# Writing five engines' instructions into the main body instead of into a block

## The chip, the cores and the metric

The kernel runs on one core of one Trainium2 chip. The metric is device time in microseconds (us); lower is better. The core has five engines that run instruction streams of their own and meet only through semaphores: TensorE (PE, with its weight loads shown as PEld), VectorE (DVE), ScalarE (ACT), GpSimd (POOL) and SyncE (SP), which here issues transfers.

## The reference, cut to what matters

Two independent problems, A and B, of the same shape are computed and their outputs laid side by side. Each is one decoding step of attention over the last 4096 positions of a cache.

```python
B, Sq, D = 2, 1, 576
Hq, Hkv, Sk, Dh = 32, 16, 16384, 128
W = min(4096, max(256, Sk // 4))                      # 4096
q = (x @ wq).reshape(B, Sq, Hq, Dh).transpose(0, 2, 1, 3)
k = jnp.repeat(k_cache[:, :, Sk - W:, :], 2, axis=1)
v = jnp.repeat(v_cache[:, :, Sk - W:, :], 2, axis=1)
p = softmax(jnp.einsum("bhqd,bhkd->bhqk", q, k) * Dh ** -0.5)
o = jnp.einsum("bhqk,bhkd->bhqd", p, v)
out = o.transpose(0, 2, 1, 3).reshape(B, Sq, Hq * Dh) @ wo     # 2 x 1 x 576
# result: concatenate([out_A, out_B], axis=-1), 2 x 1 x 1152, bfloat16
```

## The kernel before, in words

The caches are cut into slabs of 4 MB (128 partitions of 16384 bfloat16): 16 slabs of keys and 16 of values for both problems together. A ring of four slab buffers (`ring`) holds what is in flight. SP issues nearly all loads, in a written order: the two query weights `wq` (L253, L255), then key and value slabs in turn (L246), with pieces of the output weights `wo` between them (L280). A slab's load waits until the last reader of its ring slot is done. The last value slab comes in two pieces (L242).

For a key slab, DVE transposes 32x32 blocks of it (L460) and PE multiplies with the queries (L483, L167); for the softmax DVE takes the maximum (L493, L506), ACT the exponential (L528), and POOL spreads the row sums (L544). For a value slab PE multiplies (L575), and ACT copies the sums out (L587). Towards the end of each problem PE multiplies with `wo` (L690) and DVE and ACT copy the halves of the result to `out_sb` (L698, L699). Four small stores write it out (L708), three from SP's queue and one from ACT's.

The order on each engine is written out by the program itself. `S.add` appends an operation with its dependencies to the list of one engine; `S.check` walks the lists; a second walk works out which semaphore values each operation has to wait for. At the end `emit(name, engine)` turns one engine's list into instructions: the waits, the operation, and the step of that engine's semaphore. Behind its list SP also waits until the four stores have landed (`out_sem`).

Before the first of these instructions there is an opening barrier that the program object makes when it is created (L893): four engines report on one semaphore, POOL gathers them and releases them on another. The kernel opens a block (L106 to L107); each engine's list is then written by a function registered with the block (L854 to L873), so that the source has, for each engine, a jump into its part of the block and one out of it, and where the block is left (recorded under L106) a second barrier of the same kind: a DRAIN on each engine, a gathering and releasing on POOL.

Of the kernel before, what the change touches and what calls it, by code (L numbers as in the profile page):

```python
# [59 lines left out]
def build_kernel(nc, probs, out, cfg=None):  # L60
# [8 lines left out]
    NPROB = len(probs)  # L69
    Bb, _one, D = x0.shape  # L70
    _, Hkv, Sk, Dh = k0.shape
    HD = wq0.shape[1]
    Hq = HD // Dh
# [30 lines left out]

    es = ExitStack()
    with es:  # L106
        block = es.enter_context(nc.Block())  # L107
        sb = lambda name, shape, dt: es.enter_context(nc.sbuf_tensor(name, shape, dt))
        ring = sb("ring", [128, NR, SLABW], BF16)
        xt = sb("xt", [128, NKT, 2048], FP32)  # L110
# [51 lines left out]
        out_sem = sem("outdone")  # L162
# [10 lines left out]
        dma_count = {}  # L173
# [672 lines left out]
        def emit(eng_name, engine):  # L846
            for op in S.ops[eng_name]:
                for s_h, val in todo[id(op)]:
                    engine.wait_ge(s_h, val)
                last = op.fn(engine)  # L850
                if op.dma is None:
                    last.then_inc(ev[eng_name], 1)

        @block.sync  # L854
        def _(e):
            emit("sp", e)
            e.wait_ge(out_sem, dma_count[out_sem])

        @block.tensor
        def _(e):  # L860
            emit("pe", e)

        @block.vector
        def _(e):
            emit("dve", e)

        @block.scalar
        def _(e):
            emit("act", e)

        @block.gpsimd
        def _(e):
            emit("pool", e)  # L873


def bass_concat_heads__sliding_block_cached__sliding_block_cached__decode_kernel(
    nc, A_x, A_k_cache, A_v_cache, A_wq, A_wo, B_x, B_k_cache, B_v_cache, B_wq, B_wo, out,
):
    build_kernel(nc, [(A_x, A_k_cache, A_v_cache, A_wq, A_wo), (B_x, B_k_cache, B_v_cache, B_wq, B_wo)], out)
# [28 lines left out]
```

## Time and profile before

| | |
|---|---|
| median of three runs | 366.08 us |
| lowest and highest of the runs | 365.82 and 366.17 us |
| span of the profiled execution, from first to last recorded instruction of the program | 364.5 us |
| the profiled execution's own time | not listed apart from its span |
| instructions recorded | 2971 |
| mean granted TensorE clock | 0.834 of full speed |
| busy: PE, DVE, ACT, POOL | 219.7, 198.6, 67.8, 16.4 us |
| HBM read | 153.10 MB, 420 GB/s over the span |

The profile is one execution on the chip, with times counted from the first recorded instruction. The first and the last microsecond matter here, and instructions that only wait, branch or step a semaphore are not counted as busy; they are found under the line of the source that made them. "SPq" and the like stand for an engine's instruction queue. The trace also keeps the moments at which semaphores change, those of the program around the kernel too, and these lie before the zero and behind the end of the span as well.

### The profile page before, as it was taken

The page shows a single profiled execution, that of the slowest core. Times are in us where ns is not written, and L with a number is a line of the kernel's source. Part 1 is how long each engine was busy: PE and PEld are TensorE (multiplying, and loading weights), DVE is VectorE, ACT ScalarE, POOL GpSimd, SP SyncE. Part 2 cuts the span into 40 slices and gives each one's busy share as a digit, 9 for nine tenths or more (in the row PEclk, how much of TensorE's full clock was granted, in tenths as well). Part 3 has the DMA queues.
Part 4 walks back from the last instruction along what each step waited for, and adds up shares of the span by engine and source line. Part 5 has one row for each costly group of instructions (what it writes and reads, how often), then busy time and mean ns, then how long its engine had stood idle before and what let it go on. Part 6 is the DMA issues. An engine that isn't in the chain of part 4 may idle for free.

```text
span 364.5 us, 2971 instructions
## 1 busy us (share of the span) xinstructions
PE 219.7 (60%) x1370; PEld 64.7 (18%) x1097; DVE 198.6 (54%) x173; ACT 67.8 (19%) x155; POOL 16.4 (4%) x45
## 2 busy tenths in 40 slices
PE   0399687291837657192955749083764828286866
PEld 0023112020211212021211212021221202021132
DVE  2022895574909375382917568291926557199620
ACT  1047203020300303020200303020210303011211
POOL 5000000000000000000000000000000000000000
PEclk9999899697885969687685969889696969869985
DMA  8999999999999999999999999999999999999993
GB/s 345 432 432 435 428 409 457 414 453 408 440 435 428 433 412 447 424 433 428 427 445 421 442 424 424 430 432 432 422 450 421 442 421 423 439 421 442 415 419 136
DMA packets 7075, 153.27 MB, mean 420 GB/s; under 512 B 780, under 2 KB 1304, under 8 KB 1688
## 3 DMA queue, kind: packets, MB, share of 16 engines
q1 hardware_dynamic: 7056, 153.10, 98.1%
q8 instruction: 9, 0.15, 0.2%
q10 hardware_dynamic: 8, 0.00, 0.0%
q14 instruction: 2, 0.02, 0.0%
HBM read 153.10 MB, written 0.00 MB: 420 GB/s over the span
## 4 chain that ended last, share of the span: by engine, by line
DMA 70%; DVE 14%; PE 12%; ACT 2%; issue 0%; SPq 0%; DVEq 0%
DMA ring<-in_B_k_cache_dram 34%; DMA ring<-in_A_k_cache_dram 25%; DVE xt L460 13%; DMA ring<-in_B_v_cache_dram 8%; PE st L483 4%; PE st L167 3%; DMA x_sb<-in_B_x_dram 3%; PE tb L413 3%; ACT qrow L422 1%; PE tb L167 1%; DVE qtr L428 1%; PE ot L690 1%; DVE nM L506 1%; ACT qk L436 0%; PE tb L496 0%
## 5 line engine op out<-in xcount | busy, mean ns | idle before, releaser
L460 DVE STREAM_TRANSPOSE xt<-ring 128x2048 f32<-128x2048 f32 x64 | 144.9, 2285 | 108.3 <-DMA ring<-in_B_k_cache_dram 59.4
L483 PE MATMUL st<-xt,zq 128*128 128x512 bf16 x256 | 113.0, 442 | 121.5 <-DVE xt L460 121.2
L167 PE MATMUL st<-xt,zq 128*128 128x512 bf16 x256 | 111.9, 437 | 0.0
L483 PEld LDWEIGHTS st<-xt,zq 128*128 128x128 bf16 x256 | 27.3, 107 | 209.7 <-DVE xt L460 138.5
L511 ACT ACTIVATE nMrep<-nM 1x128 f32<-1x128 f32 x16 | 4.9, 308 | 176.5 <-DVE nM L506 176.5
L575 PE MATMUL acc<-ring,pC 128*32 128x512 bf16 x512 | 34.1, 403 | 1.3 <-DMA ring<-in_B_v_cache_dram 1.3
L536 DVE STREAM_TRANSPOSE pC<-pR 128x1024 bf16<-128x1024 bf16 x16 | 19.4, 1214 | 3.7 <-ACT pR L528 2.1
L587 ACT ACTIVATE acc_sb<-acc 128x512 bf16<-128x512 f32 x16 | 9.5, 596 | 62.8 <-PE acc L575 62.8
L493 DVE TENSOR_REDUCE m<-st 128x1 f32<-128x1024 f32 x16 | 19.0, 1190 | 1.0 <-PE st L167 0.9
L528 ACT ACTIVATE pR<-st,bias_sb 128x1024 bf16<-128x1024 f32 x16 | 17.8, 1113 | 0.5
L413 PE MATMUL tb<-ring,xT 128*128 128x512 bf16 x50 | 16.5, 419 | 0.1
L575 PEld LDWEIGHTS acc<-ring,pC 128*32 128x32 bf16 x512 | 13.2, 100 | 17.3 <-issue 6.2
L428 DVE STREAM_TRANSPOSE qtr<-qrow 128x512 f32<-128x512 f32 x8 | 5.7, 711 | 19.1 <-ACT qrow L422 19.1
L544 POOL TENSOR_SCALAR rsel<-maskS,rsum 128x8 f32<-128x8 bf16 x16 | 4.9, 306 | 243.1 <-ACT pR L528 243.1
L391 ACT ACTIVATE st<-maskB 128x1024 f32<-128x1024 bf16 x14 | 14.4, 1028 | 0.4
L447 POOL TENSOR_TENSOR zq<-qk,maskA 128x128 bf16<-128x128 bf16 x16 | 6.3, 398 | 86.8 <-PE st L167 69.5
L690 PE MATMUL ot<-wob,Rsb 128*2 128x288 bf16 x120 | 9.8, 309 | 0.3 <-ACT Rsb L670 0.3
L422 ACT ACTIVATE qrow<-tb 128x512 bf16<-128x512 f32 x16 | 9.2, 586 | 3.6 <-PE tb L413 3.3
L354 PE MATMUL tb<-ident_b,x_sb 4*128 4x4 bf16 x4 | 0.3, 173 | 14.8 <-DVE x_dup L361 14.8
L413 PEld LDWEIGHTS tb<-ring,xT 128*128 128x128 bf16 x50 | 5.1, 105 | 11.5 <-issue 7.5
L413 PE MATMUL tb<-wqr,xT 128*128 128x512 bf16 x16 | 6.6, 411 | 0.0
L361 DVE COPY x_dup<-x_sb 4x64 bf16<-4x64 bf16 x2 | 0.3, 190 | 11.5 <-DMA x_sb<-in_B_x_dram 11.5
(64 smaller groups left out, 83.3 us busy)
## 6 DMA issues: line engine op xcount, KB each, us to landing
ring<-in_A_k_cache_dram SPq DMA_DIRECT2D x8, 4096.0 KB, 30.5
ring<-in_A_v_cache_dram SPq DMA_DIRECT2D x8, 4096.0 KB, 35.3
ring<-in_B_k_cache_dram SPq DMA_DIRECT2D x8, 4096.0 KB, 30.7
ring<-in_B_v_cache_dram SPq DMA_DIRECT2D x7, 4096.0 KB, 35.2
wob<-in_A_wo_dram SPq DMA_DIRECT2D x4, 1152.0 KB, 37.1
ring<-in_A_wq_dram SPq DMA_DIRECT2D x1, 4096.0 KB, 12.8
ring<-in_B_wq_dram SPq DMA_DIRECT2D x1, 4096.0 KB, 21.8
wob<-in_B_wo_dram SPq DMA_DIRECT2D x3, 1152.0 KB, 37.4
```

What stands on the lines that cost most here:

```text
L167: return e.add_instruction(mybir.InstMatmult(name=nc.get_next_instruction_name(), engine=i.engine, ins=[e.lower_ap(rhs), i.ins[1]], outs=[ ...
L391: chain[(s, "fill")] = S.add("act", lambda e: e.activation(ST[s % 2][:, :].rearrange("k (h j) -> k h j", h=2), maskB[:].unsqueeze(1).broad ...
L413: last = q_first[1] = e.matmul(bank[:, 0:512], x_, w_, start=(k_ == 0), stop=(k_ == NFC))
L422: evs.append(S.add("act", lambda e, bank=bank, nb=nb: e.activation(qrow[:, 512 * nb:512 * nb + 512], bank[:, 0:512], ACTF.Copy), d, "qrow% ...
L460: Xop[(s, u)] = S.add("dve", lambda e: e.transpose(xt[:, i % NKT, :].rearrange("k (j w) -> k j w", w=64), ring[:, n % NR, :].bitcast(FP32) ...
L483: first = last = e.matmul(bank, zq[:, p4, s % NZQ, w0:w0 + 128], mv, start=False, stop=stop, skip_group_check=True)
L493: chain[(s, "max")] = S.add("dve", lambda e: e.tensor_reduce(m1[:, 0:1], ST[s % 2][:, :], AX.X, ALU.max), d, "max%d" % s)
L528: chain[(s, "exp")] = S.add("act", lambda e: e.activation(pR[:, :], ST[s % 2][:, :], ACTF.Exp, bias=bias_sb[:, 0:1], scale=SCALE, accum_ou ...
L536: chain[(s, "pC")] = S.add("dve", lambda e: e.transpose(pC[:, s % NPT, :, :].rearrange("k j c -> k (j c)"), pR[:, :]), d, "pC%d" % s)
L575: last = e.matmul(ACC[32 * cb:32 * cb + 32, 0:512], pC[:, D_ % NPT, j0_:j0_ + 4, :].rearrange("k j c -> k (j c)"), ring[:, n % NR, j0_ * 1 ...
L587: acc_ev[D_] = S.add("act", lambda e: e.activation(acc_sb[:], ACC[:, :], ACTF.Copy), d, "accev%d" % D_)
L690: last = e.matmul(proj_out(half), l_, wob[:, pc, s_, half * NH:(half + 1) * NH], start=False, stop=True, skip_group_check=True)
```

## The change

The block is not opened. `emit` is called five times with the engines themselves, so that their instructions go into the main body; SP's wait for the stores stands behind its list as before. The opening barrier of the program object (L893) stays.

```diff
     es = ExitStack()
     with es:
-        block = es.enter_context(nc.Block())
         sb = lambda name, shape, dt: es.enter_context(nc.sbuf_tensor(name, shape, dt))
...
-        @block.sync
-        def _(e):
-            emit("sp", e)
-            e.wait_ge(out_sem, dma_count[out_sem])
-
-        @block.tensor
-        def _(e):
-            emit("pe", e)
-
-        @block.vector
-        def _(e):
-            emit("dve", e)
-
-        @block.scalar
-        def _(e):
-            emit("act", e)
-
-        @block.gpsimd
-        def _(e):
-            emit("pool", e)
+        emit("sp", nc.sync)
+        nc.sync.wait_ge(out_sem, dma_count[out_sem])
+        emit("pe", nc.tensor)
+        emit("dve", nc.vector)
+        emit("act", nc.scalar)
+        emit("pool", nc.gpsimd)
```

## The prediction

> **What bounds the kernel now.** I read four views: the page, the chain of waits, and the instructions of the two lines that belong to the barriers (L893, where the program object is made, and L106, where the block closes). The page first:
>
> ```profile
> span 364.5 us, 2971 instructions
> ...
> DMA  8999999999999999999999999999999999999993
> ...
> q1 hardware_dynamic: 7056, 153.10, 98.1%
> q8 instruction: 9, 0.15, 0.2%
> ```
>
> The transfers of queue q1 fill 98.1% of sixteen engines' span: the kernel streams 153 MB and everything between about 1 and 358 us is set by that. Nothing in the change touches a transfer, so what is to be looked at are the two ends. The chain that ended last, its first and last pieces (start, length, what):
>
> ```profile
> 0.73 0.07 issue
> 0.79 0.40 SPq L253
> 1.25 0.42 SPq L255
> 1.72 12.56 DMA x_sb<-in_B_x_dram
> ...
> 358.32 1.07 PE acc L575 x7
> ...
> 360.34 2.03 PE ot L690 x16
> ...
> 362.39 0.45 DVE out_sb L698
> ```
>
> SP's first load is issued at 0.79 us, 0.07 us after the opening barrier let SP go, and a delay there would move the whole stream. At the other end the last computed tile is ready at 362.84; then come the stores and the close. The close, all instructions of L106 (duration min/median/max in ns, first and last start in us):
>
> ```profile
> L106 POOLq EVENT_SEMAPHORE  x2: 17/17/17, 364.3 to 364.4; - x2
> L106 POOLq DRAIN  x1: 422/422/422, 346.8 to 346.8; - x1
> L106 PEldq DRAIN  x1: 1283/1283/1283, 361.1 to 361.1; - x1
> ...
> L106 SPq COMPARE_BRANCH  x1: 33/33/33, 364.1 to 364.1; - x1
> L106 SPq DRAIN  x1: 13/13/13, 364.3 to 364.3; - x1
> ...
> L106 PEldq EVENT_SEMAPHORE  x1: 51/51/51, 364.5 to 364.5; - x1
> ```
>
> SP's wait for the four stores ends at 364.1 in its COMPARE_BRANCH; SP's DRAIN reports to POOL, POOL gathers and releases, and all engines leave at 364.5. Between 364.1 and 364.5 nothing else runs: this stretch is exposed, and it ends the span. The queue's own waits show the same two pieces:
>
> ```profile
> SPq L106 <- DMA out_dram<-out_sb: 1.0, 1, 1.0
> ...
> SPq L106 <- PEq L106: 0.2, 1, 0.2
> ```
>
> The first, 1.0 us for the stores, stays; the second goes.
>
> **The change part by part.** Each engine's compute and DMA instructions, and their waits, are the same in the same order on both sides. What differs is at the ends.
>
> *Entry branches, five of them.* The source has a jump into each engine's block (L854, L859, L863, L867, L871), but the trace has no instruction on any of these lines; the one branch in it is SP's COMPARE_BRANCH at the close, which carries the wait for the stores. So I take the entry branches as already gone. Bound: SP's release (L893) starts at 0.711 and takes 0.017, and its first load starts at 0.794, a gap of 0.066 us; the smallest gaps between two loads on SP's queue, with no branch between, are 0.042. At most 0.024 us is left for a branch, at the least nothing; I take 0, since no record stands there. [...]
>
> *Closing barrier, on L106.* Removed are one COMPARE_BRANCH, five DRAINs and six EVENT_SEMAPHOREs (four engines one each, POOL two); added is one EVENT_SEMAPHORE on SP that holds the wait for the stores. 2971 − 12 + 1 = 2960 instructions. On the path to the end lie only SP's branch and DRAIN, POOL's gather and release and the engines' leaving. In the records at full resolution the branch starts at 364.128 and PE leaves at 364.512. The new wait ends where the branch started and takes 0.017, as SP's other EVENT_SEMAPHORE does, so SP's program ends at 364.145: the span is 364.512 − 364.145 = 0.367 us shorter, 364.1 in place of 364.5. The other four DRAINs are free: POOL's ends at 347.2, PE's and DVE's before 362.9, ACT's at 363.4, all covered by the stores' landing up to 364.11; with that cover gone they are removed anyway.
>
> *What the close was covering: the meeting behind it.* The trace keeps changes of semaphores outside the span too. Behind 364.512 semaphore 2, which the kernel does not own, is stepped nine times: 364.751, 364.785, 364.997, 365.041, 365.064, 365.162, 365.202, 365.236, 365.282. Just ahead of the span there are nine such steps as well, ending at 0.000. I read it as a line of five engines, up and back, each adding one when the engine before it has. The way back gives the order: behind the steps at the start the engines begin in the order SP 0.000, DVE 0.123, POOL 0.135, ACT 0.142, PE 0.315 (within 0.02 for the three in the middle), and behind those at the end five blocks of some 50 semaphores are cleared, beginning at 365.182, 365.298, 365.342, 365.352 and 365.499. So SP is the turning point, the fifth step (365.064), and PE the first (364.751), 0.239 behind its own release, which ended at 364.512.
>
> Before the change all five are let go within 0.09 us (POOL 364.424, SP 364.466, ACT 364.470, DVE 364.481, PE 364.512), so the line going up starts at zero: PE's 0.239, a step of 0.034, a step of 0.212 in which the third engine (POOL, by that order, 0.573 behind its release) is awaited, two short ones, and it reaches SP at 365.064. After the change four engines are done long before SP: POOL 347.2, PE 362.4, DVE 362.8, ACT 363.1. Even with 0.573 each they stand in line by 363.7. What is late next is SP alone: its step comes its own lead behind 364.145, and the way back (0.218) follows as now.
>
> SP's lead isn't shown, since its step waited for DVE's. Bounds: PE's 0.239 from its release is the plain lead, POOL's 0.573 the longest seen, and zero the least. Nearest are rows where SP and PE do the same thing: from their step to the clearing of semaphores SP took 0.118 and PE 0.217; from their step to the first instruction at the start SP 0.231 and PE 0.315. That is 0.54 and 0.73 of PE's, so SP's lead comes to 0.13 to 0.17; I take 0.15 as an estimate. Then SP steps at 364.145 + 0.15 = 364.295, where it was 365.064: a gain of 0.77 us in all, 0.37 of it inside the span and 0.40 behind it. With a lead of 0.239 it is 0.68, with none 0.92, with 0.573 it is 0.35. What follows (clearing to 365.85, a second line to 366.53) hangs on the first and moves with it.
>
> From the last release to the ninth step the meeting takes 365.282 − 364.512 = 0.77 us. [...]
>
> *The body.* Ahead of the close no recorded instruction goes or comes on any engine, so nothing has a reason to start at another time, the nine q8 instruction reads included. Cost 0.
>
> **Sum.** The profiled execution is known by its span, 364.5; its own time isn't listed. The median of the runs is 366.08, 1.57 us above the span, which is about the close counted above and the opening steps. I subtract from the median: 366.08 − 0.77 = 365.31.
>
> A measurement of this kernel can tell about 0.2%, 0.73 us, from no change: faster means under 365.35, slower over 366.81. My gain stands just over that line, so the chances on both sides of it are near each other.
>
> **The rivals.**
>
> *SP comes to the meeting as slowly as POOL does* (lead 0.573). Then the meeting absorbs what the engines gained and only about the barrier's own stretch comes off: 366.08 − 0.35 = 365.73, within 0.2%. [...] Against: SP is the quicker of the two in both rows where they can be compared.
>
> *The change does nothing for the measured time*: the meeting behind the program was the true end and has a fixed length from another event, so the close only moves idle time. 366.08. Against it: the meeting's first step follows PE's release by 0.239, as a dependent would, and its later one (366.072) follows PE's last cleared semaphore (365.847) by 0.225.
>
> [...] If the gap of 0.066 us were all branch and SP's lead zero, 0.92 + 0.07 = 0.99: 365.09. [...]
>
> *Slower: instruction reads come uncovered.* The nine q8 reads of 16 KB take 1.02 to 1.10 us each and are hidden now. Were their position shifted against the work by writing the engines' streams into one body, PE would stand for one read at a time. One on the chain gives 366.08 − 0.77 + 1.07 = 366.38, still the same; it decides from two on, 366.08 − 0.77 + 2.14 = 367.45. For it: PE sits near the chain in every slab (L483 and L167 hold 7% of it). Against: each engine's own order and count ahead of the close is unchanged, and DMA, not PE, fills the slab.
>
> **How the numbers follow.** The forecast has 0.62, of which 0.45 falls under 365.35 and 0.17 above (lead of 0.24, or the runs' scatter of 0.35 us from lowest to highest); SP as slow as POOL 0.16; no effect 0.07; the larger gain 0.08; slower 0.07. Faster: 0.45 + 0.08 = 0.53. Same: 0.17 + 0.16 + 0.07 = 0.40. Slower 0.07. The range reaches from the larger gain with the scatter below it, 364.9, to the slow SP with scatter above it, 366.0; no effect and slower lie outside, 0.14 together.
>
> **What would show it.** In the profile after: 2960 instructions; no COMPARE_BRANCH and no DRAIN at the close; SP's last EVENT_SEMAPHORE at about 364.1 as the last instruction, and a span of 364.1 against 364.5; the first load still at about 0.79. Four engines' steps of semaphore 2 long before SP's, and SP's 0.15 behind its wait. If the span shrinks by 0.4 and the time by no more, SP's lead was underestimated; if the span shrinks by much more than 0.4, or the first load comes earlier, the entry held a cost that I took for nothing; if the span doesn't shrink, or the stores land later, the body moved, and the reasoning on it is wrong.

## The result, and the profile after

The changed kernel takes 364.81 us (median of 12 runs), the kernel before in the same comparison 365.97 (12 runs): ratio 0.997, 95% interval 0.9962 to 0.9978, so 1.16 us or 0.3% faster. When both were measured again (first experiments below) the difference was 0.99 us, ratio 0.9978 (0.9968 to 0.9989). The direction was forecast; the size was forecast as 0.77, and the time lies 0.09 us below the range.

The page of the changed kernel:

```profile
span 363.2 us, 2960 instructions
...
q1 hardware_dynamic: 7056, 153.10, 98.4%
q8 instruction: 9, 0.15, 0.2%
```

The instruction count is the forecast one. Lines of the kernel are numbered one lower than before, since one line near its top is gone; L854 is now SP's wait for the stores. The chain that ended last, its first and last pieces (start, length, what):

```profile
0.73 0.07 issue
0.80 0.40 SPq L252
...
358.10 0.64 PE acc L574 x8
...
361.46 0.45 DVE out_sb L697
```

The first load starts at 0.80 us: the records read 0.795 where they read 0.794, so the entry held no cost. The close is one instruction (duration min/median/max in ns, first and last start in us), and the wait that it ends is the same 1.0 us:

```profile
L854 SPq EVENT_SEMAPHORE  x1: 17/17/17, 363.2 to 363.2; - x1
```

```profile
SPq L854 <- DMA out_dram<-out_sb: 1.0, 1, 1.0
```

**A trap in this pair of profiles.** The spans differ by 1.3 us, which looks like the whole gain. It isn't: 0.93 of it lies ahead of the close. By the two chains, the piece of the last value slab landed 0.22 earlier (358.06 against 358.28), and the work from there to the copies into `out_sb` took 0.71 less (3.40 against 4.11); that part goes with the TensorE clock. Busy times of 357 to 363 us, with the granted clock third from the right, for the kernel before, for its repeat, for the changed kernel and for its repeat:

```profile
357.00:363.00 6.00, 4.45 (x42) 1.40 (x34) 0.61 (x2) 1.18 (x3) 0.00 (x0) 0.50 0.28 101
```

```profile
357.00:363.00 6.00, 3.62 (x46) 1.29 (x38) 0.61 (x2) 1.18 (x3) 0.00 (x0) 0.89 0.25 89
```

```profile
357.00:363.00 6.00, 2.80 (x34) 0.95 (x30) 0.61 (x2) 1.18 (x3) 0.00 (x0) 0.77 0.26 93
```

```profile
357.00:363.00 6.00, 4.38 (x42) 1.34 (x30) 0.61 (x2) 1.18 (x3) 0.00 (x0) 0.50 0.25 90
```

Half clock fell on the tail in the first profile of the kernel before, and just as well in the repeat of the changed kernel, whose span was then 364.0 against 363.5 for the repeat of the kernel before. So the prediction's sign for a hidden cost at the entry, a span that shrinks by much more than 0.4, can't be read from this pair. Medians over runs say what the change does to the span: 363.6 before (30 runs), 363.2 and 363.3 after. The rest of the gain is outside: time minus span is 2.30 us before (median of the 30) and 1.62 after.

The nine steps up and back that the prediction reads as a line of engines are called the first line from here on, and the nine behind them, from 366.072 to 366.530 before, the second line. In the changed kernel (the trace's records, us; the bars stand around SP's step):

```
first line:   361.601  362.512  362.551  362.595 | 363.342 | 363.387  363.425  363.459  363.506
second line:  364.295  364.329  364.367  364.412 | 364.435 | 364.907  364.945  364.979  365.026
```

Four engines stand in the first line before SP's wait ends at 363.215; SP steps 0.127 later, and the way back takes 0.164. That is the picture that the prediction drew. What it did not draw is the second line, in which the step behind the turning point now comes after 0.472 instead of 0.099. By the order of the line that is VectorE's step on the way back.

### The profile page after: what moved, and what is told of

Same layout as the page of the kernel before. It is cut to its first block, busy times and chain, and to the rows that moved or that the text cites. A ratio compares the mean times of both kernels' runs of the same rounds, so it can differ in the third digit from the quotient of the medians.

```text
span 363.2 us, 2960 instructions
## 1 busy us (share of the span) xinstructions
PE 220.4 (61%) x1370; PEld 64.6 (18%) x1097; DVE 198.7 (55%) x173; ACT 67.8 (19%) x155; POOL 16.4 (5%) x45
## 4 chain that ended last, share of the span: by engine, by line
DMA 70%; DVE 14%; PE 12%; ACT 2%; issue 0%; SPq 0%; DVEq 0%
DMA ring<-in_B_k_cache_dram 34%; DMA ring<-in_A_k_cache_dram 25%; DVE xt L459 13%; DMA ring<-in_B_v_cache_dram 8%; PE st L482 4%; PE st L166 4%; DMA x_sb<-in_B_x_dram 3%; PE tb L412 3%; ACT qrow L421 1%; PE tb L166 1%; DVE qtr L427 1%; DVE nM L505 1%; ACT qk L435 0%; PE ot L689 0%; PE tb L495 0%
## 5 line engine op out<-in xcount | busy, mean ns | idle before, releaser
L482 PE MATMUL st<-xt,zq 128*128 128x512 bf16 x256 | 114.6, 448 | 119.9 <-DVE xt L459 119.9
L166 PE MATMUL st<-xt,zq 128*128 128x512 bf16 x256 | 113.0, 441 | 0.0
L574 PE MATMUL acc<-ring,pC 128*32 128x512 bf16 x512 | 32.8, 391 | 1.3 <-DMA ring<-in_B_v_cache_dram 1.2
L505 DVE TENSOR_REDUCE nM<-tb 1x8 f32<-1x128 f32 x16 | 4.4, 273 | 4.1 <-PE tb L495 4.1
```

The costliest lines, as they stand in the source:

```text
L166: return e.add_instruction(mybir.InstMatmult(name=nc.get_next_instruction_name(), engine=i.engine, ins=[e.lower_ap(rhs), i.ins[1]], outs=[ ...
L482: first = last = e.matmul(bank, zq[:, p4, s % NZQ, w0:w0 + 128], mv, start=False, stop=stop, skip_group_check=True)
L574: last = e.matmul(ACC[32 * cb:32 * cb + 32, 0:512], pC[:, D_ % NPT, j0_:j0_ + 4, :].rearrange("k j c -> k (j c)"), ring[:, n % NR, j0_ * 1 ...
```

## The experiments

The table counts from the profiled executions: A is from the start of the instruction that ends SP's wait to the end of the span, B from there to the last step of the first line, and C is the rest of that execution's time − span. The trace does not show where the measured time starts, so only differences of C between kernels mean something. "2nd" is from the last step of the first line to the last step of the second. "Read" marks kernels with a late read: an instruction read of 8 KB on queue q14 that starts 1.7 to 2.2 us behind the end of the span; the others have none there. "Time − span" and "time" are medians over runs. (us)

```
kernel                            A     B     C   2nd  read  time-span     time
before, again                  0.38  0.77  1.48  1.25   yes       2.31   365.91
changed                        0.02  0.29  1.32  1.52             1.62   364.81
changed, again                 0.02  0.29  1.32  1.52             1.63   364.94
barrier without block          0.28  0.77  1.57  1.25   yes       2.37   365.74
four engines wait              0.06  0.79  1.10  1.15             1.90   365.24
POOL waits                     0.02  0.83  1.33  1.51             2.20   365.40
TensorE waits                  0.06  0.55  1.46  1.51             1.89   364.97
VectorE waits                  0.03  0.39  0.96  1.15             1.36   364.60
one DRAIN on each              0.01  0.29  1.10  1.15             1.41   364.58
VectorE +1 DRAIN               0.02  0.28  0.97  1.16             1.25   364.57
VectorE +1 DRAIN, again        0.02  0.29  0.96  1.15             1.27   364.49
VectorE +2                     0.02  0.28  1.07  1.25             1.35   364.42
TensorE +2                     0.02  0.29  1.32  1.52             1.59   364.91
POOL +3                        0.02  0.29  1.33  1.52             1.61   365.05
SP +1                          0.07  0.28  1.33  1.52             1.66   364.94
ScalarE +2                     0.02  0.29  1.64  1.52             1.93   365.18
ScalarE +2, VectorE +1         0.02  0.29  1.51  1.18   yes       1.83   365.18
before's counts, no barrier    0.07  0.28  1.61  1.24   yes       1.84   364.96
```

A kernel's time − span stays within about 0.1 us of its median from run to run (within 0.15 where TensorE waits, 0.2 in the kernels with the read), while the span scatters by several tenths; so it is the former that tells these kernels apart.

**Is the gain inside the span, behind it, or chance?** The kernel before unchanged:

> The kernel before, once more, to see its spans run by run. Theory M (the engines' meeting behind the program is part of the measured time): time minus span is about 2.0 us here and 1.6 in the changed kernel, so 0.4 of the gain lies behind the span. Theory S (the measured time follows the span, what is outside is constant): time minus span is 1.6 in both, and the spans themselves differ by 1.1 us, of which the close explains 0.37. Theory N (chance): the times of this repeat scatter so far that the 1.16 us shrink, under S to about 0.4. Time under M and S 366.0, under N anything from 365.2 to 366.0.

Time − span is 2.31: theory M, and 0.68 above the changed kernel, more than its 0.4. And the changed kernel unchanged:

> The changed kernel once more. M and S: 364.8 again, span 363.2. N: between 364.8 and 365.6. In the trace, if the full clock of TensorE in the last 5 us was chance, the tail's products of the last value slab may now take 1.07 us as before instead of 0.64.

364.94, and the chance clock as foreseen. N and S are out.

**Barrier or branches?** The barrier put back, the block not:

```diff
         emit("pool", nc.gpsimd)
+        nc.all_engine_barrier()
```

> No block and no branches, but the same closing barrier (a DRAIN on each engine, gathering and release by POOL) behind the instructions. If the barrier alone is the cause, this is the kernel before: M 365.6 to 366.0, with a span 0.35 longer than the changed kernel's and 0.5 us more behind the span. S with the barrier as whole cause: 365.2, span 0.35 longer. If the branches or labels of the block are what costs, this stays at 364.8 plus 0.35.

365.74, ratio to the kernel before 0.9996 (0.9987 to 1.0005): the barrier brings the time back, and with it the late read. The close of this kernel, where the wait is on an instruction of its own (L854) and the barrier is L859:

```profile
L859 SPq DRAIN  x1: 7/7/7, 363.3 to 363.3; - x1
L859 SPq EVENT_SEMAPHORE  x1: 17/17/17, 363.5 to 363.5; - x1
...
L859 PEldq EVENT_SEMAPHORE  x1: 51/51/51, 363.5 to 363.5; - x1
```

A is 0.276 here and 0.379 with the block: the one branch that survives costs 0.103 us more than the plain wait does, since SP's DRAIN starts 0.164 us behind its start and only 0.061 behind the start of the plain wait. The other branches cost nothing that shows.

**Does it matter when engines come to the line?** All four made to wait for the stores:

```diff
+        for e in (nc.tensor, nc.vector, nc.scalar, nc.gpsimd):
+            e.wait_ge(out_sem, dma_count[out_sem])
```

> No block and no barrier, but the four other engines also wait for the four stores at their end, so that all five come to the meeting behind the program at once. The span stays within 0.05 us of the changed kernel's. M: the line of engines starts only then and reaches SP about 0.5 us later, time 365.3. S: 364.85, since only what is inside the span counts.

```profile
L860 ACTq EVENT_SEMAPHORE  x1: 17/17/17, 363.3 to 363.3; - x1
L860 POOLq EVENT_SEMAPHORE  x1: 17/17/17, 363.3 to 363.3; - x1
```

B is 0.79 again, as with the barrier, and the time 365.24, near M's 365.3. But C fell from 1.32 to 1.10, which no theory had, so that time − span rose by 0.28 where B alone would have made it 0.5; that the time agrees with M is in part chance. One engine at a time (`nc.gpsimd`, `nc.tensor` or `nc.vector` alone in the loop above):

> The changed kernel, in which POOL alone also waits for the four stores. Theory L with POOL as the slow one: its step in the line comes 0.57 us behind its wait, so the first line ends where it did with four engines waiting, and the whole 0.3 us comes back: time minus span 1.9, time 365.2. If POOL's arrival does not matter: 1.6 and 364.9.

POOL's is the third step and comes 0.54 us behind its wait; time − span 2.20, where 1.9 was expected, since C did not fall this time.

> The changed kernel, in which TensorE alone also waits for the four stores. Theory L: TensorE is first in the line, steps 0.24 us behind its wait and the line then runs up and back in 0.37 without waiting for anyone, so it ends 0.61 behind the wait where it was 0.31: up to 0.3 later, time 365.1 to 365.2. If only the slow POOL counts, 1.6 and 364.9.

TensorE's is the first step, 0.19 behind its wait; B is 0.55 and time − span 1.89, so 0.27 more, as theory L has it (up to 0.3). The time of 364.97 lies below L's 365.1, but with the scatter of the spans it doesn't decide.

> The changed kernel, in which VectorE alone also waits for the four stores. Theory L: VectorE stands next to the turning point; with a lead like SP's (0.13) the line ends 0.05 later, with one like POOL's (0.57) 0.4 later. Time minus span 1.65 to 2.0, time 364.9 to 365.3. In the first line its step shows which.

VectorE's is the fourth step, 0.15 behind its wait. B rises by 0.1, near the 0.05 foreseen for a quick engine, but the time *falls*, to 364.60: C is 0.96. So a late arrival costs what the line shows, and something else gains 0.36. In the steps it is the second line: its last step comes 1.150 us behind that of the first, where it takes 1.520 in the changed kernel and 1.246 in the kernel before.

**What shortens the second line?** One DRAIN at the end of each engine:

```diff
+        for e in (nc.sync, nc.tensor, nc.vector, nc.scalar, nc.gpsimd):
+            e.drain()
```

> The changed kernel with a DRAIN at the end of each engine (SP's holds the wait for the stores), and no gathering or release. So far the time from the end of SP's wait on is 1.63 us in the changed kernel, 1.95 with four engines waiting for the stores, 2.62 with the barrier. Theory L (what counts is when engines come to the line behind the program): four engines still come early, so 1.63 to 1.70, time 364.9, time minus span 1.6. Theory D (the DRAINs themselves make the program's close behind the span longer): up to 2.3, time 365.5.

364.58, under both theories' numbers; the second line is 1.151. This kernel, the one in which VectorE waits and the one in which four engines wait have one instruction more on VectorE's stream, and all three have a second line of 1.15. The next four add DRAINs alone, at the end of an engine, so that nothing comes later than SP:

```diff
+        for e, n in ((nc.vector, 1),):     # or (nc.tensor, 2), (nc.vector, 2), ...
+            for _ in range(n):
+                e.drain()
```

> The changed kernel with one DRAIN more, on VectorE alone, at its end and long done before the stores land. So far the end behind the span falls into steps: the second line of engines takes 1.15 us with one instruction more on VectorE, 1.52 without, whether VectorE came late or not. Theory C (the number of instructions on an engine's stream sets how long its part of the close behind the program takes): second line 1.15, time minus span 1.25, time 364.45, faster than the changed kernel by 0.37. Theory A (only when engines arrive counts): nothing arrives later or earlier, so 1.62 and 364.8 to 364.9.

> The changed kernel with two DRAINs more on VectorE alone. Theory C: the second line takes 1.245 us, as in the kernel before, which has two more on VectorE too; time minus span 1.34, time 364.55. Theory A: 1.62, 364.8 to 364.9.

Time − span 1.25 and 1.35, second line 1.155 and 1.249: theory C to the hundredth in both, while the times of 364.57 and 364.42 miss its 364.45 and 364.55 by 0.12 to either side, within the spans' scatter. An instruction that ends 1.2 us before SP's wait does takes 0.36 us off time − span; a wait on VectorE, which ends with SP's, does the same to C. The line of that DRAIN in the repeat of the first kernel:

```profile
L859 DVEq DRAIN  x1: 484/484/484, 361.4 to 361.4; - x1
```

> The changed kernel with two DRAINs more on TensorE alone, at its end. Theory C: the time's end lies 0.19 us ahead of the second line's last step in the changed kernel, 0.05 ahead with one instruction more on TensorE, 0.25 to 0.33 behind it in the kernel before, which has two more; if TensorE's count is what does it, time minus span is 2.05 to 2.1 and the time 365.3. Theory A: 1.62, 364.8 to 364.9.

Nothing (1.59): the two instructions more that the barrier puts on TensorE are not what makes the time end later.

> No barrier, but as many instructions on each engine as the kernel before has: DRAINs at each engine's end (two on TensorE, VectorE and ScalarE, three on POOL, one more on SP behind its wait). Theory C: the first line as in the changed kernel (ends 0.3 us behind the span), the second 1.245, the time's end 0.3 behind that, and a late 8 KB instruction read as in both kernels with the barrier: time minus span 1.85, time 365.05. Theory A: 1.62 to 1.7, 364.9.

Time − span 1.84, C 1.61: without any barrier, C is near that of the kernels with one, and the late read is there. The DRAINs of this kernel:

```profile
L861 POOLq DRAIN  x3: 34/41/424, 346.8 to 347.3; - x3
L861 PEldq DRAIN  x2: 13/280/547, 360.8 to 361.4; - x2
L861 DVEq DRAIN  x2: 19/252/484, 361.4 to 361.9; - x2
L861 ACTq DRAIN  x2: 8/128/247, 362.1 to 362.4; - x2
L861 SPq DRAIN  x2: 7/7/7, 363.1 to 363.2; - x2
```

On SP the count is one short: the kernel before has 57 instructions recorded there, the changed kernel 55, and this one 56. The other four engines have what they had before.

**Which engine's count?** The same lines for `nc.scalar` twice, `nc.gpsimd` three times, `nc.sync` twice (the first DRAIN carries SP's wait, so one more):

> The changed kernel with two DRAINs more on ScalarE alone. With the kernel before's count on every engine the late 8 KB instruction read is there and the time ends 0.37 us behind the second line; TensorE's and VectorE's two do not bring it. If ScalarE's count does: the late read, the end 0.25 to 0.37 behind the second line instead of 0.2 ahead, time minus span 2.1 to 2.2, time 365.3 to 365.4. If not: 1.6 and 364.9.

> The changed kernel with three DRAINs more on POOL alone, the kernel before's count. If POOL's count brings the late read: time minus span 2.1 to 2.2, time 365.3 to 365.4. If not: 1.6 and 364.9.

> The changed kernel with SP's wait on a DRAIN and a second DRAIN behind it, so one instruction more on SP, the kernel before's count. If SP's count brings the late read: time minus span 2.1 to 2.2, time 365.4. If not: 1.6 and 364.9; the first line starts 0.06 later with respect to SP's wait.

ScalarE's: C rises to 1.64, though without the late read, and somewhat less than expected (time − span 1.93). Three more on POOL and one more on SP do nothing (1.61, 1.66). How the two counts combine:

```diff
+        for e, n in ((nc.scalar, 2), (nc.vector, 1)):
```

> The changed kernel with two DRAINs more on ScalarE and one more on VectorE. Alone the first put the time's end 0.32 us later, the second 0.36 earlier, counted from the last step of the first line (1.32 in the changed kernel, 1.64 and 0.97 with the one and the other). Theory P (two parallel paths, the longer one counts): ScalarE's path hides VectorE's, so 1.6 again, time minus span 1.9, time 365.1 to 365.2. Theory Q (the two add up): 1.29, time minus span 1.57, time 364.8. P would also explain the kernel before, with 1.5 to 1.6, without anything left over.

C is 1.51 and time − span 1.83, between the two numbers but nearer to P's: of the 0.36 that VectorE's instruction brings alone, 0.1 is left. Theory P has the nearer number, but its picture of two paths isn't shown: the second line is short (1.18), and the late read is there, which neither change brings alone.

**A version with a shorter stretch behind the span.** The changed kernel with one DRAIN on VectorE:

```diff
         emit("pool", nc.gpsimd)
+        nc.vector.drain()
```

> The changed kernel with one DRAIN more on VectorE alone, again, beside the three others, as the version that should beat both kernels: second line 1.15 us, time minus span 1.25, time 364.5, against 364.8 to 364.9 of the changed kernel and 365.95 of the kernel before.

364.49 us, ratio to the kernel before 0.9965 (0.9951 to 0.9979), 0.9959 (0.9947 to 0.9971) when it ran first. Against the changed kernel the intervals of the times overlap; time − span is 1.27 against 1.62 and does not.

## Why the prediction was right or wrong

*Entry branches at nothing: right.* No record, and the first load at 0.795 us where it was at 0.794. The 0.07 us for a branch there, which the larger gain counts and with it the lower end of the range, shows in no run.

*The closing barrier, 0.367 inside the span: right.* A went from 0.379 to 0.017. It is made of 0.26 for the barrier and 0.10 for SP's branch, which the prediction did not part.

*The line of engines behind the program: right in kind, a little small.* SP's lead was 0.127 (taken 0.15), and the way back 0.164 (taken as the old 0.218). B went from 0.77 to 0.29: 0.48 for a predicted 0.40. The order of steps was read rightly: holding TensorE, POOL or VectorE moved the first, third or fourth.

*"What follows hangs on the first and moves with it": the step that failed.* Its own change was put at zero. The second line does start 0.79 behind the first in both kernels, but what comes then isn't rigid: by the medians C went from 2.30 − 0.77 = 1.53 to 1.62 − 0.29 = 1.33, a gain of 0.20. The barrier had put two or three instructions on each engine. ScalarE's two are worth 0.3 us of C by themselves, and with VectorE's they bring the late read; taking VectorE's two away lengthens the second line by 0.27 and gives part back. With the 0.08 of the line, 0.77 becomes 0.36 + 0.48 + 0.20 = 1.04, between the 0.99 and the 1.16 that were measured.

*Why the time fell below the range.* The mis-sized terms alone would have put the forecast at 366.08 − 1.04 = 365.04, still inside. The other 0.23 is scatter: the kernel before came out at 365.97 in this comparison, 0.11 lower, and the difference was 0.12 larger than the parts. The repeat's 364.94 lies inside.

*The base.* I paired the span of 364.5 with the median of 366.08 and took 1.57 us to lie outside. It is 2.30: that execution, with half clock in its tail, was longer than the median (364.5 + 2.3 would be 366.8). The sum did not use the 1.57, but read rightly it would have shown that more of the time lies outside the span than the sum had accounted for.

*The rivals.* SP's slowness and no effect are out by B and by the barrier put back. Slower by instruction reads: the nine q8 reads start within 1.3 us of where they did, and none shows on the chain. But a count of instructions does act at the end of the program (one more on VectorE 0.36 us less, two more on ScalarE 0.3 more), where the prediction had counted four of the removed DRAINs as free.

*What the late read does to the time.* In the four kernels with the read whose execution has a time of its own, the read lasts 0.31 to 0.47 us, and its end lies 0.30 us (0.299 to 0.307) behind the point that this time reaches when it is counted from the profile's zero. The second line's last step keeps no such distance (0.23 to 0.37 ahead of that point). So in these kernels the measured time moves with the end of the read, though no run changed the read alone, and the read's own length goes far to explain the spread of C between 1.48 and 1.61; by the medians C is 1.54 to 1.60 in all four.

*Left open.* Why a count acts so. The instructions of the close behind the program aren't recorded, nor the event that ends the measured time; only semaphores and reads are. The late 8 KB read goes with two more on ScalarE and one or two more on VectorE (both kernels with a barrier, before's counts, ScalarE +2 with VectorE +1), not with either alone, and not with one more on each. No run here explains why C is as high as 1.64 with ScalarE's two alone, where there is no late read, or why it is 0.14 higher with one instruction more on each engine than with VectorE's alone. TensorE's may be the one: its wait alone shows 0.14 in the profiled execution, but not in the median of its six runs.

## What to carry to other kernels

The barrier at the end of the program was paid twice here: 0.26 us inside the span (A of 0.28 with it, 0.02 without), and 0.48 behind it (B of 0.77 and 0.29), where engines that were let go together stood in line one after the other. So I would let all but one engine run out early and leave the last wait to the engine that is quickest there, here SP (0.13 us from its wait to its step, POOL 0.54), whose step is also the turning point. Read time − span over several runs before you read two spans: in most kernels here it stayed within 0.1 us of its median, while one profile's span was 0.9 above the median, mostly through the clock of its tail. At a level of 0.1%, try one idle instruction more or less on an engine: here one on VectorE moved time − span by 0.36 us, about what the close took off the span (0.367).

## What the runs showed of the hardware that I had not expected

The engines' leads from the end of a wait to their step in the line: SP 0.13, VectorE 0.15, TensorE 0.19, POOL 0.54 us. Time − span by instructions added at an engine's end: one on VectorE's stream, 0.36 us less; two, 0.27 less; two on ScalarE's, 0.3 more; two on TensorE's, three on POOL's, one on SP's, nothing. Where an instruction read of 8 KB comes behind the program, the measured time kept the same distance from the end of that read (0.299 to 0.307 us in four kernels).
